# A fused SSM convolution and token-mixing MLP on one core: the hand-over from the last convolution chunk to the first four w1 blocks, rearranged

## The chip, the core and the metric

The kernel runs on one core of a Trainium2 chip. A core has a matrix engine (TensorE, "PE" in the profile, its weight loads "PEld"), VectorE ("DVE"), ScalarE ("ACT"), GpSimd ("POOL") and SyncE ("SP", here the queue that issues nearly all DMAs). Each engine works through its own queue in order. SBUF is the working memory of 128 partitions; PSUM receives the matmuls' results, here as four slots of two banks each (`pst0` to `pst3`). The metric is the time of one execution in microseconds (us), lower is better.

## The reference

One batch, S = 2048 tokens, D = 640 channels, F = 1728 hidden units, all float32:

```python
mod = (silu(c) @ w_mod)                       # six rows of 640: sa, ca, ga, sb, cb, gb
h = layernorm(x) * (1 + ca) + sa              # x = A_q, over the channels
kv = shift_conv(A_k, 4 taps) * A_v
y = causal_conv(kv, A_ssm_k) + kv * A_ssm_D   # length 2048, by FFT of length 4096, per channel
x = x + ga * (h * y)
h = layernorm(x) * (1 + cb) + sb
u = gelu(einsum("bsd,sf->bdf", h, w1) + b1)   # over the tokens
x = x + gb * (einsum("bdf,fs->bds", u, w2) + b2).transpose
```

## The kernel before

**First half.** The convolution works on five chunks of 128 channels (loop over `c`, L503). A chunk's transform has two stages in (`step1`, L208; `f2`, L222, eight groups g, multiplied with the kernel's transform by VectorE's `mul` and GpSimd's `add` into `Y`) and two stages out (`i2`, L253, two calls into `T2`, which lies in the tile `z`; `i1`, L268, two calls, one for each half of the 16 token rows j). A token row j is 128 tokens, one for each partition; `XH`/`XR(j)` (L83) hold x, rows 0 to 7 in tile `xa`, 8 to 15 in `xb`. `a1_ops` (L281) makes the first norm's rows in `A1` (ScalarE `ac`, then VectorE `po`), `gate` (L294) multiplies them with the result of `i1` in PSUM and adds to x, `spill` (L301) writes the chunk of x to DRAM (`xs`) for the end of the kernel. While `c` is worked on, `fill` holds loose VectorE work for the next chunks; in the last ones it is the statistics of finished chunks (`x1s`).

**Modulation.** `c @ w_mod` takes five pieces of 128 rows for three of the six rows at a time: `mod_load` (L339), `mod_part` (L343, six matmuls a piece, each two instructions, accumulated in `tap`, slot 3), `mod_sum` (L350) to SBUF, `mod_row` (L354), which spreads a row over the partitions and stores it (3: shift `SB`, 4: scale `CB`, 5: gate `GB`).

**Second half.** The first products contract over the tokens: `h` of the 16 rows j against w1 in 14 blocks of 128 hidden units. To reach float32 accuracy each operand is split in two parts of the type fp32r, `hi` (ScalarE copy) and `lo` (VectorE subtraction): `split_w` (L404) for weights, `H[j]` for h, and `mm` (L418) makes three products (hi hi, hi lo, lo hi), each in two halves of 320 columns, so six matmuls for a row and a block. Blocks 0 to 3 are accumulated together, row pair by row pair, since h comes into being only then; blocks 4 to 13 run afterwards on the finished `H`, one after the other (L796). Blocks then go through `u_evac` (L743), and the w2 products follow.

**Order around the change.** Everything is in the order written (`manual_schedule`, L53). In the last chunk (`c` = 4, `cn` None) after f2: the last two modulation pieces are loaded into `z`; block 0 (loaded in chunk 3 to `X`) is split, then `po`, three `mod_part`s, loads of blocks 1 to 3 (`aux`, `p`, `x`), `i2(0)`, splits of blocks 1 and 2, `i2(1)`, the last two `mod_part`s, split of block 3, load of block 4, `mod_sum`, `i1(0)`, `gate` of half 0, `i1(1)`, `mod_row(4)` and `(3)`. A w1 block is loaded by `load_w` (L390) for 128 columns of all 16 rows, 512 bytes at a time. Then (L698 on) the rows go through, a pair pr at a time: `x1_stats` (L659), a root by `rstd` (L308) or `rstd_pool` (L321: ScalarE's Sqrt, then a Newton step on GpSimd), `norm1` (ScalarE, into one of six pieces `tmp`), `mod_stats` (L668: times `CB`, plus `SB`, and the second norm's statistics, on VectorE), again `rstd_pool`, `norm2` (L678: the normed row and its `hi`), `rests` (its `lo`) and `products` (L691). The first norm's statistics are made for rows 0, 1, then 2 to 7, then 8 to 15 in one go each.

PSUM tiles come from `psum()` (L69), which goes round slots 0 to 2 in the first half and 0 to 3 from L655 on; a new tile on a slot, and a new tile on a memory tag (`mem`), waits until everything on the old one is done.

Of the kernel before, what the change touches and what calls it, by code (L numbers as in the profile page):

```python
# [49 lines left out]
def mixer_kernel(ctx: ExitStack, tc: tile.TileContext, q, k, v, shift_k, ssm_k, ssm_D, w1, b1, w2, b2, c,  # L50
# [16 lines left out]
    ring = [3]  # L67

    def psum():  # L69

        uid[0] += 1
        return psp.tile([128, 1024], F32, name=f"pst_{uid[0]}", tag=f"pst{uid[0] % ring[0]}", bufs=1)
# [9 lines left out]
    T_g, T_rows, T_t, sm = mem("g", 1280), mem("rows", 640), mem("t", 1280), mem("sm", 704)  # L82
# [24 lines left out]
    def small(n):  # L107
        so[0] += n
        assert so[0] <= 704
        return sm[:, so[0] - n:so[0]]  # L110
# [7 lines left out]
    msk = small(1)  # L118
    epsc = small(1)
# [133 lines left out]
    def i2(r):  # L253
# [9 lines left out]
        for qd in range(4):  # L263
            act.activation(T2[:, 8 * qd + 4 * r:8 * qd + 4 * r + 4].rearrange("p a m e -> p a e m"),
                           pp[qd // 2][:, 512 * (qd % 2):512 * (qd % 2) + 512].rearrange("p (a e m) -> p a e m",
                                                                                         a=4, e=2), AF.Copy)

    def i1(half):  # L268

        ps = psum()  # L270
# [10 lines left out]
    def a1_ops(c):  # L281
# [5 lines left out]
        if c == 0:  # L287
            def scaled(h):
                a, gh = A1[:, 8 * h:8 * h + 8], lambda G: G[:, None, 0:DC].to_broadcast([128, 8, DC])
# [4 lines left out]
    def gate(c, ps, half, eng=pool):  # L294
        a = A1[:, 8 * half:8 * half + 8]
        av = a.rearrange("p j (m e) -> p e j m", e=2)
        TT(dve, av, ps.rearrange("p (e j m) -> p e j m", e=2, j=8), av, ALU.mult)
        x = XH[half][:, :, DC * c:DC * c + DC]
        TT(eng, x, x, a, ALU.add)

    def spill(c):  # L301
        for half in range(2):
# [5 lines left out]
    def rstd(r, nm, j0, n):  # L308
# [3 lines left out]
        dve.tensor_scalar(v_, v_, EPS, None, op0=ALU.add)  # L312
        act.activation(t_, v_, AF.Sqrt)
        dve.reciprocal(r_, t_)
        TT(dve, t_, r_, r_, ALU.mult)
        TT(dve, t_, t_, v_, ALU.mult)
        dve.tensor_scalar(t_, t_, -0.5, 1.5, op0=ALU.mult, op1=ALU.add)
        TT(dve, r_, r_, t_, ALU.mult)
        dve.scalar_tensor_tensor(nm_, m_, -1.0, r_, op0=ALU.mult, op1=ALU.mult)

    def rstd_pool(r, nm, j0, n, between=None):  # L321

        m_, v_ = mv[:, j0:j0 + n, 0], mv[:, j0:j0 + n, 1]
        r_, nm_, t_ = r[:, j0:j0 + n], nm[:, j0:j0 + n], tm[:, j0:j0 + n]
        e_ = bst[:, j0:j0 + n, 4, 0]
        act.activation(t_, v_, AF.Sqrt, bias=epsc)
        pool.tensor_scalar(e_, v_, EPS, None, op0=ALU.add)
        pool.tensor_scalar(m_, m_, -1.0, None, op0=ALU.mult)
        if between:
            between()  # L330
        dve.reciprocal(r_, t_)
        TT(pool, t_, r_, r_, ALU.mult)
        TT(pool, t_, t_, e_, ALU.mult)
        pool.tensor_scalar(t_, t_, -0.5, 1.5, op0=ALU.mult, op1=ALU.add)
        TT(pool, r_, r_, t_, ALU.mult)
        TT(pool, nm_, m_, r_, ALU.mult)
# [17 lines left out]
    def mod_row(i, t):  # L354

        ps, j = psum().rearrange("p (h m) -> p h m", h=2), i % 3
# [4 lines left out]
        two = lambda t: t.rearrange("p (h m) -> p h m", h=2)  # L361
        if i == 0:
# [40 lines left out]

    def split_w(i, t2=None, eng=dve):  # L404
# [13 lines left out]
    def mm(ps, wh, wl, rh, rl, first, last):  # L418
# [581 lines left out]
```

## Time and profile before

| what | value |
|---|---|
| three runs | 741.24 us median, 734.45 to 748.20 |
| profiled execution | 737.33 us, span 735.5 us, mean granted TensorE clock 0.955 |
| PE busy | 653.1 us (89%) |
| PEld busy | 630.5 us (86%) |
| DVE busy | 499.4 us (68%) |
| ACT busy | 299.5 us (41%) |
| POOL busy | 176.2 us (24%) |
| last f2 ends, first four w1 blocks end | 288.1 us, 404.4 us |

How to read it. The page shows one execution; times are us from the span's start, durations in group rows mean ns of one instruction. A row of a group or of the timeline reads: line, engine, operation, tile written <- tiles read, shape, count, busy time; in brackets or behind the bar the idle time in front of it and who ended it. Most VectorE and GpSimd work goes through the helper on L59, so those rows are told apart by their tiles. The float32 matmuls of the first half count as two instructions each, fp32r ones (L424) as one. "PEclk" is the share of full clock that TensorE was granted.

### The profile page before, as it was taken

What the parts mean: (1) busy time and instruction counts of PE and PEld (TensorE: products, weight loads), DVE (VectorE), ACT (ScalarE), POOL (GpSimd) and SP (SyncE); (2) the same over time, 40 slices, a digit from 0 to 9 for tenths busy, and PEclk for the clock granted to TensorE, in tenths of its full rate; (3) what the DMA queues carried; (4) which work ended last, traced back from release to release, by engine and by line L of the source; (5) the groups of instructions that cost most, each with busy time, mean ns of one, the idle gap of its engine ahead of it and who ended that gap; (6) DMA issues with size and microseconds to landing.
All of it is one profiled execution on the core that took longest, in us unless ns stands there. A gap on an engine that the chain in (4) does not pass through costs nothing.

```text
span 735.5 us, 20693 instructions
## 1 busy us (share of the span) xinstructions
PE 653.1 (89%) x9107; PEld 630.5 (86%) x9107; DVE 499.4 (68%) x857; ACT 299.5 (41%) x441; POOL 176.2 (24%) x176
## 2 busy tenths in 40 slices
PE   0797969999999989655899999999999989999997
PEld 0787749989989978544899999999999989999997
DVE  7756659969877548488994321231298958888886
ACT  0432465645646535425665512321235322333222
POOL 5197048626329047022440000000000000000000
PEclk9999889999999999657899999999999999999999
DMA  9989988445420174950000535335163333555410
GB/s 180 241 235 255 265 228 167 97 80 132 89 61 4 29 198 151 187 116 2 0 1 21 95 77 96 58 59 110 55 186 101 92 117 110 153 164 172 145 55 36
DMA packets 171921, 84.90 MB, mean 115 GB/s; under 512 B 88852, under 2 KB 165431, under 8 KB 171831
## 3 DMA queue, kind: packets, MB, share of 16 engines
q1 hardware_dynamic: 167282, 82.26, 45.5%
q10 hardware_dynamic: 4548, 1.31, 1.1%
q8 instruction: 71, 1.16, 0.7%
q14 instruction: 20, 0.16, 0.1%
HBM read 73.07 MB, written 10.49 MB: 114 GB/s over the span
## 4 chain that ended last, share of the span: by engine, by line
PE 58%; DVE 22%; issue 6%; DMA 4%; POOL 4%; ACT 3%; SPq 2%; ACTq 0%; DVEq 0%; POOLq 0%
PE pst L424 26%; PE pst L216 9%; PE pst L941 7%; PE pst L232 6%; DVE m_w L59 4%; PE pst L261 4%; POOL y L59 3%; PE pst L277 3%; DVE m_x L59 3%; DVE tap L59 3%; DVE kt L59 2%; ACT m_w L854 2%; PE pst L866 2%; DVE m_x L875 1%; DVE m_v L59 1%
## 5 line engine op out<-in xcount | busy, mean ns | idle before, releaser
L232 PE MATMUL pst<-z,w 128*64 128x64 f32 x2560 | 96.8, 241 | 11.7 <-ACT z L218 6.1
L232 PEld LDWEIGHTS pst<-z,w 128*64 128x64 f32 x2560 | 95.3, 142 | 13.6 <-ACT z L218 7.3
L424 PE MATMUL pst<-r_z,wb 128*128 128x320 f32 x504 | 82.9, 321 | 16.4 <-ACT r_z L685 11.3
L59 POOL TENSOR_TENSOR y<-p 128x256 f32<-128x256 f32 x72 | 90.4, 1304 | 26.8 <-DVE p L59 26.6
L424 PEld LDWEIGHTS pst<-r_z,wb 128*128 128x128 f32 x504 | 79.1, 198 | 18.3 <-ACT r_z L685 12.5
L59 DVE TENSOR_TENSOR p<-pst,kt 128x512 f32<-128x512 f32 x80 | 52.7, 690 | 28.5 <-ACT kt L236 19.3
L216 PE MATMUL pst<-v,x 128*64 128x128 f32 x640 | 46.0, 303 | 23.6 <-DVE x L59 23.6
L218 ACT ACTIVATE z<-pst 128x1024 f32<-128x1024 f32 x40 | 45.8, 1146 | 48.6 <-PE pst L216 28.4
L216 PEld LDWEIGHTS pst<-v,x 128*64 128x64 f32 x640 | 44.0, 221 | 24.2 <-POOL t L449 23.6
L424 PE MATMUL pst<-h_x,wb 128*128 128x320 f32 x336 | 51.1, 309 | 0.0
L424 PEld LDWEIGHTS pst<-h_x,wb 128*128 128x128 f32 x336 | 49.7, 188 | 0.0
L236 ACT ACTIVATE kt<-pst 128x512 f32<-128x512 f32 x40 | 25.2, 630 | 59.4 <-PE pst L232 38.8
L261 PEld LDWEIGHTS pst<-v,y 32*128 32x128 f32 x1280 | 42.6, 204 | 6.8 <-issue 2.6
L261 PE MATMUL pst<-v,y 32*128 32x64 f32 x1280 | 44.7, 291 | 4.2 <-DVE y L59 1.4
L746 ACT ACTIVATE pst<-pst,sm 128x640 f32<-128x640 f32 x14 | 10.7, 767 | 86.1 <-PE pst L424 86.1
L59 DVE TENSOR_TENSOR wb<-x,wb 128x1024 fp32r<-128x1024 f32 (+1 forms) x32 | 36.8, 1188 | 12.0 <-ACT wb L413 11.9
L866 PE MATMUL pst<-r_z,m_w 128*128 128x320 f32 x222 | 42.8, 312 | 1.9 <-DVE m_w L59 1.4
L216 PE MATMUL pst<-v,p 128*64 128x128 f32 x640 | 37.8, 274 | 2.4 <-issue 2.4
L854 ACT ACTIVATE m_w<-m_v 128x896 fp32r<-128x896 f32 x24 | 22.2, 950 | 42.4 <-DVE m_v L59 29.5
L424 PE MATMUL pst<-h_a,wb 128*128 128x320 f32 x252 | 38.8, 309 | 0.0
L424 PE MATMUL pst<-r_v,wb 128*128 128x320 f32 x252 | 38.8, 309 | 0.0
L216 PEld LDWEIGHTS pst<-v,p 128*64 128x64 f32 x640 | 35.2, 137 | 3.6 <-issue 3.2
(213 smaller groups left out, 1272.2 us busy)
## 6 DMA issues: line engine op xcount, KB each, us to landing
x<-in_B_w_dram SPq DMA_DIRECT2D x24, 512.0 KB
m_v<-in_B_w_dram SPq DMA_DIRECT2D x15, 384.0 KB
x<-in_B_w_dram SPq DMA_DIRECT2D x14, 384.0 KB
aux<-in_A_ssm_k_dram SPq DMA_DIRECT2D x10, 512.0 KB
in<-in_A_k_dram SPq DMA_DIRECT2D x36, 128.0 KB
in<-in_A_v_dram SPq DMA_DIRECT2D x36, 128.0 KB
m_x<-xs SPq DMA_DIRECT2D x28, 160.0 KB
out_dram<-m_x SPq DMA_DIRECT2D x28, 160.0 KB
```

What stands on the lines that cost most here:

```text
L59: TT = lambda eng, o, a, b, op: eng.tensor_tensor(o, a, b, op=op)
L216: pe.matmul(ps[64 * ri:64 * ri + 64, o:o + 128], lhs, F1[:, 128 * ri:128 * ri + 128], start=True, stop=True)
L218: evac = lambda: act.activation(Z[:, side, t].rearrange("p a k e -> p e a k"), ps.rearrange("p (e a k) -> p e a k", a=8, e=2), AF.Copy)
L232: pe.matmul(ps[64 * h:64 * h + 64, o:o + 64], W2[k1 // 32][:, 2 * (k1 % 32) + ri], rhs, start=True, stop=True)
L236: act.activation(kt.rearrange("p (m i) -> p m i", i=32), pv[:, :, 1], AF.Copy)
L261: pe.matmul(pp[qd // 2][:, o:o + 64], Y[p, ri, i:i + 2].rearrange("p i k -> p (i k)"), V2[p, 64 * ri:64 * ri + 64], start=ri == 0, stop=ri ...
L277: pe.matmul(ps[64 * b:64 * b + 64, 512 * e + 64 * jj:512 * e + 64 * jj + 64], V1[p, ri, n2], T2[p, :, 32 * ri + n2], start=ri == 0, stop=r ...
L424: pe.matmul(ps[0:m, h, 0:320], w_.bitcast(F32R), r_[:, 320 * h:320 * h + 320].bitcast(F32R), start=first and i == 0, stop=last and i == 2)
L746: act.activation(p, p, AF.Gelu_apprx_tanh, bias=B1C[:, f:f + 1])
L854: act.activation(W[n][0].bitcast(F32R), a(w_), AF.Copy)
L866: pe.matmul(bank[n], w[:, i].bitcast(F32R), r.bitcast(F32R), start=i == 0 and k == 0, stop=i == 6 and k == 2)
L941: pe.matmul(acc[s][:, h, 0:320], w[:, f_].bitcast(F32R), u[r + h].bitcast(F32R), start=f_ == 0 and k == 0, stop=f_ == NF - 1 and k == 2)
```

## The change

It rearranges the last chunk and the four blocks; the computation and the number of w1 matmuls stay the same.

1. **Weights by rows.** `load_rows(r)` loads four token rows j = 4r to 4r+3 of blocks 0 to 3 at once, 2048 bytes at a time; `split_rows` splits them for chosen blocks. Rows 0 to 7 are loaded in chunk 3, rows 8 to 15 after the first half's gate, split in the pair loop. Blocks 0 and 1 take tiles `w0`, `w1`, block 3 `in`, block 2 `y`.
2. **Modulation.** Two pieces are loaded in chunk 3 instead of three; the third and fourth go to `z`, the fifth to `p`, all issued after f2. The third `mod_part` still stands ahead of `i2(0)`, the fourth stands between the two `i2`, the fifth after `i1(0)`. `CB` is stored by VectorE; `SB`'s ScalarE copy also sums it (`msb`).
3. **Last chunk's order.** The po of the last chunk is by halves, two of its four passes inside f2's groups 5 and 6. Two of the four copies of `i2(1)` go to VectorE. `i1(0)` is followed by the gate of rows 0 and 1 alone, their statistics, then the gate of rows 2 to 7; `i1(1)` comes after `mod_row(4)` and `(3)`, its gate after the second pair's products have begun.
4. **Second norms by sums.** Instead of bn_stats: a fused multiply by `CB` with a running sum gives the mean (`second`), a fused add subtracts it and adds `SB`, a ScalarE Square with a running sum gives the variance. The Square's result goes to the place of the row's `lo` and is overwritten. The normed row isn't stored any more: `hi` and `lo` are made from the centred row with the root as scale.
5. **Roots in one pass.** The roots of the second norm of a pair and of the first norm of a later pair are taken together (`root_in`: GpSimd and ScalarE; `root`: VectorE, Newton step in four instructions, `newton`).
6. **Products.** For pairs 0 to 6 the products with `hi` of both rows for all blocks come first, then those with `lo`; pair 0 leaves block 3 for later. Rows from 4 on are normed in place in x instead of `tmp`; statistics of later rows are made two or four at a time.

```diff
     def i2(r, eng=None):
...
+            if eng is not None and qd > 1:
+                eng.tensor_scalar(o, i, 1.0, None, op0=ALU.mult)
+            else:
+                act.activation(o, i, AF.Copy)
...
+    def newton(r, t, v, n=None):
+        dve.reciprocal(r, t)
+        dve.scalar_tensor_tensor(t, r, -0.5, r, op0=ALU.mult, op1=ALU.mult)
+        TT(dve, t, t, v, ALU.mult)
+        dve.scalar_tensor_tensor(r, t, 1.5, r, op0=ALU.add, op1=ALU.mult)
...
+    def load_rows(r, t):
+        for i in range(4):
+            sync.dma_start(t[:, 512 * i:512 * i + 512], dram(w1, (4 * r + i) * F, [[16 * F, 2], [32 * F, 64], [1, 512]]))
+
+    def split_rows(r, t, blocks, hi=True, lo=True):
+        j, t = slice(4 * r, 4 * r + 4), t.rearrange("p (j m) -> p j m", j=4)
+        for f in blocks if hi else ():
+            act.activation(blk[f][0][:, j].bitcast(F32R), t[:, :, 128 * f:128 * f + 128], AF.Copy)
+        for f in blocks if lo else ():
+            TT(dve, blk[f][1][:, j].bitcast(F32R), t[:, :, 128 * f:128 * f + 128], blk[f][0][:, j], ALU.subtract)
...
+            if cn is None and g in (5, 6):
+                run(po[:1])
+                po = po[1:]
...
         else:
-            for kk in range(3, 5):
-                mod_load(3, kk, pl[kk])
-            split_w(0)
-            run(po)
+            mod_load(3, 2, pl[2])
+            mod_load(3, 3, pl[3])
+            mod_load(3, 4, pl[4])
             for kk in range(3):
                 mod_part(tap, kk, three(pl[kk]))
-            load_w(1, T_aux[:, 0:2048])
-            load_w(2, P)
-            load_w(3, X)
+            split_rows(0, X, (0, 1, 3))
+            split_rows(1, T_aux[:, 0:2048], (0, 1, 3))
+            run(po)
...
             i2(0)
             if cn is None:
-                split_w(1)
-                split_w(2, mem("in", 4288, "wb2"))
+                mod_part(tap, 3, three(pl[3]))
+                i2(1, dve)
+                split_rows(0, X, (2,))
+                split_rows(1, T_aux[:, 0:2048], (2,))
+                break
...
+            pl = [T_in[:, 0:1920], T_in[:, 1920:3840], T_z[:, 0:1920], T_z[:, 1920:3840], P[:, 0:1920]]
+            for kk in range(2):
+                mod_load(3, kk, pl[kk])
+            load_rows(0, X)
+            load_rows(1, T_aux[:, 0:2048])
...
+    roots = (((), (0, 1)), ((0, 1), (2, 3)), ((2, 3), (4, 5)), ((4, 5), (6, 7, 8, 9)), ((6, 7), (10, 11)),
+             ((8, 9), (12, 13)), ((10, 11), (14, 15)), ((12, 13), ()), ((14, 15), ()))
...
+    def root_in(n):
+        second_, first_ = roots[n]
+        o = start[n]
+        if second_:
+            pool.tensor_scalar(V_[:, o:o + 2], V_[:, o:o + 2], 1 / D, EPS, op0=ALU.mult, op1=ALU.add)
+            o += 2
+        if first_:
+            pool.tensor_scalar(V_[:, o:start[n + 1]], mv[:, first_[0]:first_[-1] + 1, 1], EPS, None, op0=ALU.add)
+        act.activation(T_[:, start[n]:start[n + 1]], V_[:, start[n]:start[n + 1]], AF.Sqrt)
...
+    def second(pr):
+        for j in (2 * pr, 2 * pr + 1):
+            t = row(j)
+            dve.scalar_tensor_tensor(t, t, 1.0, CB, op0=ALU.mult, op1=ALU.mult, accum_out=su[:, j:j + 1])
+        n = su[:, 2 * pr:2 * pr + 2]
+        dve.tensor_scalar(n, n, msb, -1 / D, op0=ALU.add, op1=ALU.mult)
+        for j in (2 * pr, 2 * pr + 1):
+            t = row(j)
+            dve.scalar_tensor_tensor(t, t, su[:, j:j + 1], SB, op0=ALU.add, op1=ALU.add)
+        for j in (2 * pr, 2 * pr + 1):
...
+            act.activation(H[j][1].bitcast(F32R), row(j), AF.Square, accum_out=at(V_, 2, j))
+
+    def halves(pr):
+        for j in (2 * pr, 2 * pr + 1):
+            act.activation(H[j][0].bitcast(F32R), row(j), AF.Identity, scale=at(R_, 2, j))
+
+    def rests(pr):
+        for j in (2 * pr, 2 * pr + 1):
+            dve.scalar_tensor_tensor(H[j][1].bitcast(F32R), row(j), at(R_, 2, j), H[j][0], op0=ALU.mult, op1=ALU.subtract)
...
+    ps0 = i1(0)
+    mod_part(tap, 4, three(pl[4]))
+    gate(NC - 1, ps0, 0, dve, 0, 2)
+    x1_stats(range(2))
+    mod_sum(tap, T_t[:, 0:640])
+    root_in(0)
+    gate(NC - 1, ps0, 0, dve, 2, 8, (lambda: root(0),))
+    spill(NC - 1, (0,))
+    mod_row(4, T_t[:, 0:640], s2)
+    norm1(0)
+    mod_row(3, T_t[:, 0:640], 3)
+    ps = i1(1, s1)
+    gb = mod_row(5, T_t[:, 0:640], s2, True)
...
+    for r, t in ((2, X), (3, P)):
+        load_rows(r, t)
+    second(0)
+    x1_stats(range(2, 4))
+    root_in(1)
+    gb()
+    root(1)
+    halves(0)
+    norm1(1)
+    rests(0)
+    products(0, range(3))
+    x1_stats(range(4, 6))
+    second(1)
+    gate(NC - 1, ps, 1, dve, then=(lambda: root_in(2), lambda: root(2), lambda: halves(1), lambda: norm1(2)))
+    spill(NC - 1, (1,))
+    products(0, [3])
+    rests(1)
+    products(1)
+    second(2)
+    x1_stats(range(6, 10))
+    root_in(3)
+    root(3)
+    halves(2)
+    norm1(3)
+    rests(2)
+    norm1(4)
+    products(2)
+    split_rows(2, X, range(4))
+    for pr in range(3, 8):
+        second(pr)
+        if pr > 3:
+            rests(pr - 1)
+            products(pr - 1)
+        if pr == 5:
+            split_rows(3, P, range(4))
+        if pr < 6:
+            x1_stats(range(2 * pr + 4, 2 * pr + 6))
+        root_in(pr + 1)
+        root(pr + 1)
+        halves(pr)
+        if pr < 6:
+            norm1(pr + 2)
+        if pr == 3:
+            load_w(4)
+    rests(7)
     products(7)
```

More of the change, by code (lines that the diff above doesn't have):

```diff
@@ L361, in mod_row @@
         two = lambda t: t.rearrange("p (h m) -> p h m", h=2)
+        if later:
+            return lambda: act.activation(two(GB), ps, AF.Copy)
         if i == 0:
@@ L618, in mixer_kernel @@
             ps = i1(half)
[L619 to L621 removed]
+            if c and half:
                 dv(3)
```

243 lines of the change are left out of this document (98 added, 145 removed).

## The prediction

> **What bounds the kernel now.** I read the page's slices first, then the chain that ended last, then the timeline of each engine and the busy time by stretches, for 286 to 405 us. The slices show where TensorE is neither busy nor at full clock: slices 16 to 19 of 18.4 us, some 294 to 368 us.
>
> ```profile
> PE   0797969999999989655899999999999989999997
> PEclk9999889999999999657899999999999999999999
> ```
>
> The chain, in order of time (start, length, what), names what ends each wait there.
>
> ```profile
> 293.01 3.39 SPq L396
> 296.44 8.34 DMA p<-in_B_w_dram
> 304.79 3.01 issue
> 307.88 2.00 ACT wb L413 x2
> ...
> 311.96 6.55 PE pst L277 x255
> ...
> 321.30 0.18 DVE sm L314
> ...
> 352.49 87.58 PE pst L424 x576
> ```
>
> So the second `i2` is computed by 304.2, but its copies out of PSUM stand on ScalarE behind the splits of w1 blocks 1 and 2, which wait for loads issued only at 291 to 299; `i1` starts at 311.96. Then VectorE's rows carry the chain, and from 352.49 TensorE is the bound: what starts its products earlier is worth something, what VectorE does beside them is not, while it keeps up. TensorE's own rows:
>
> ```profile
> 288.06 2.35 PE L347 MATMUL tap<-in,sm 128*32 128x320 f32 x24
> 291.42 4.09 PE L261 MATMUL pst<-v,y 32*128 32x64 f32 x132
> 304.11 4.00 PE L347 MATMUL tap<-z,sm 128*32 128x320 f32 x24
> 338.40 8.46 PE L424 MATMUL pst<-r_z,wb 128*128 128x320 f32 x46 [0.96 <-DVE r_z L59]
> 352.49 6.23 PE L424 MATMUL pst<-r_z,wb 128*128 128x320 f32 x22 [4.23 <-DVE r_z L59]
> 379.76 10.74 PE L424 MATMUL pst<-r_z,wb 128*128 128x320 f32 x72
> 404.42 2.80 PE L424 MATMUL pst<-r_z,wb 128*128 128x320 f32 x18
> ```
>
> The four blocks are 384 matmuls: 50 before 352.49, the rest until block 4 starts at 404.42. At full clock one takes 10.74/72 = 0.149 us, so a pair of rows (48) 7.16 us; at 352.49 it takes 0.283. Busy time in windows of 3.41 us shows why (second column PE busy, then weight load, DVE, ACT, POOL; then the granted clock):
>
> ```profile
> 293.83:297.24 3.41, 2.40 (x85) 2.27 (x80) 3.38 (x3) 1.92 (x4) 0.00 (x0) 1.00 1.14 272
> 297.24:300.65 3.41, 3.18 (x60) 2.99 (x57) 1.13 (x1) 0.26 (x1) 0.00 (x0) 0.50 1.21 204
> 304.07:307.48 3.41, 3.41 (x24) 1.32 (x24) 2.16 (x2) 0.72 (x1) 0.00 (x0) 0.50 1.21 205
> 307.48:310.89 3.41, 0.63 (x9) 0.02 (x3) 1.93 (x2) 3.01 (x5) 0.00 (x0) 1.00 0.93 162
> ```
>
> The clock is 1.00 or 0.50 through a whole window, set by the window before: 2.40 us busy lost it, 3.18 (of `i2`) didn't bring it back, 3.41 did.
>
> **The change, part 1: up to `i1(0)` in PSUM.** Before, VectorE gets it at 315.71; call that t0.
>
> ```profile
> 315.71 1.23 DVE L59 TENSOR_TENSOR aux<-pst,aux 128x1024 f32<-128x1024 f32 x1 [0.28 <-PE pst L277]
> 253.73 2.10 PE L277 MATMUL pst<-z,v 64*64 64x64 f32 x128
> 310.29 1.62 ACT z L264 x3
> ```
>
> Removed: the ScalarE queue's wait for w1. The rows of w1 for j 0 to 7 (2.1 MB) are issued behind the third spill, with two modulation loads instead of three and instead of block 0: 4.1 MB instead of 4.0, from about 268 on, needed from 289.5. SP is idle after them until 288.18, so they cost nothing there. Added: the third modulation piece now goes to `z`, which f2 reads until 288.06, and TensorE must have it before `i2(0)`; before, it lay in `aux` long since. Everything behind it on TensorE waits.
>
> ```profile
> 288.18 0.90 SPq L340 DMA_DIRECT2D z<-in_w_mod_dram  x2
> 289.00:292.46 3.46, 3.46 (x65) 1.92 (x60) 3.46 (x5) 2.49 (x4) 1.54 (x2) 1.00 0.90 285
> 294.90:300.10 5.20, 4.20 (x96) 4.06 (x92) 3.44 (x2) 2.17 (x4) 0.00 (x0) 0.73 1.20 208
> 302.78 2.00 ACT L413 ACTIVATE wb<-aux 128x1024 fp32r<-128x1024 f32 x2 [5.28 <-DMA aux<-in_B_w_dram]
> ```
>
> The first 0.98 MB of such a load have moved by 292.46 (last column: 285 GB/s). How long after its last byte a load can be used: w1's block 1 (1.05 MB at 208 GB/s behind the two z loads) has moved by 300.1 and is used at 302.78, 2.7 us. The ends are 1 and 2.7; I take 2.7, the only row: 295.2. TensorE idles from 290.4 (its two ready pieces done) to 295.2 and loses its clock at 293.83. Then twelve matmuls of the piece, 2.0 us (24 in 4.00), to 297.2; `i2(0)`, 128 matmuls at 4.09/132 = 0.031 us, twice that at half clock. The window from 297.24 is wholly busy, so I let the clock return at 300.65, as it did at 307.48: 57 matmuls cold, 71 warm, done at 302.9. The fourth piece, 1.2, goes beside ScalarE's copies (0.54 each); `i2(1)` 4.1, to 308.1; its four copies, now two on ScalarE and two on VectorE, 1.35 instead of 2.1; `i1(0)`, 128 matmuls, 2.1. So t0 = 311.6, or 4.1 earlier. Ends: cold throughout, 295.2 + 24.1 (2.0 + 7.6 + 2.0 + 7.6 + 1.4 + 3.5) = 319.3; never cold and the piece usable at 293.5, 293.5 + 13.9 = 307.4. [...]
>
> Hidden here: the splits of blocks 0, 1, 3 (six of 512 elements on each engine, done by 296), the two VectorE passes of po put into f2's last turns (they delay f2's last sums by some 0.4) and the other two (by 298.5): cover is the wait until 295.2. If that went, 0.5 us. The load into `p` waits on SP for those sums; nothing is queued behind it until the spill.
>
> **Part 2: from t0 to the first product.** Before, 22.7 us (338.40 - 315.71). Prices of one instruction:
>
> ```profile
> L59 DVE TENSOR_TENSOR t_g<-t_g,kt 128x640 f32<-128x640 f32 x12 | 9.8, 813 | 0.2
> L875 DVE SCALAR_TENSOR_TENSOR m_x<-m_x,sm 128x320 f32<-128x320 f32 x6 | 3.3, 545 | 0.0
> L59 DVE TENSOR_TENSOR m_x<-m_x 128x320 f32<-128x320 f32 x35 | 17.2, 492 | 1.2
> L59 DVE TENSOR_TENSOR wb<-x,wb 128x1024 fp32r<-128x1024 f32 x24 | 28.4, 1222 | 11.0 <-ACT wb L413 10.9
> L59 DVE TENSOR_TENSOR p<-pst,kt 128x512 f32<-128x512 f32 x80 | 52.7, 690 | 28.5 <-ACT kt L236 19.3 <-POOL y L59 8.8 <-POOL aux L59 0.3
> L662 DVE BATCH_NORM_AGGREGATE sm<-sm 128x2 f32<-128x30 f32 x16 | 4.7, 292 | 0.6
> L502 DVE BATCH_NORM_STATS2 sm<-xb 128x6 f32<-128x128 f32 x40 | 8.8, 271 | 0.0
> L666 ACT ACTIVATE t_g<-xa,sm 128x640 f32<-128x640 f32 x2 | 1.7, 912 | 4.9 <-POOL sm L59 4.9
> L685 ACT ACTIVATE r_v<-t_p 128x640 fp32r<-128x640 f32 x2 | 1.5, 743 | 0.1
> L327 POOL TENSOR_SCALAR sm<-sm 128x2 f32<-128x2 f32 x6 | 4.1, 683 | 24.9 <-DVE sm L676 24.9
> ```
>
> A fused pass of 640 elements: 0.81 plus 0.05 (545 - 492), 0.86; where it also sums, the trace has no row: as without (0.74, back to back) to 1.5 if it went at half rate; I take 0.86, next to the fused row. A small one 0.2, a root on VectorE (four steps and the mean) 1.0, statistics of a row 0.48 (0.27 + 0.29, overlapping), a Square between L685 and L666, 0.80. `second` of a pair is then 4 x 0.86 + 0.2 = 3.6, `rests` 1.6.
>
> In us after t0: gate of two rows 0.9, statistics 1.85, ScalarE's sum of the pieces and root 2.85, VectorE's root (after the gate's product for the other six) 3.9, norm of pair 0 until 5.7; row 4 (the scale), evacuated on VectorE, 5.65; `second(0)` to 9.25; Squares to 10.1 (`z` is free only when `i1(1)` has read it, about 8.5); GpSimd's sum and ScalarE's root 10.95; VectorE's root 12.0; first half 12.7. The first product is at 12.7 instead of 22.7, since the big gate(1), six rows' statistics and GpSimd's chain of five no longer stand in front of it.
>
> **Part 3: the pace behind it.** Before, VectorE has a pair done every 6.96 us, under TensorE's 7.16:
>
> ```profile
> 353.15 1.68 DVE L59 TENSOR_TENSOR t_p<-t_p,kt 128x640 f32<-128x640 f32 x2
> 360.11 1.68 DVE L59 TENSOR_TENSOR t_g<-t_g,kt 128x640 f32<-128x640 f32 x2
> ```
>
> After, a pair costs VectorE 3.6 + 1.6 + 0.95 (statistics of two later rows, before the stream before) + 1.0 = 7.15, and eight splits of 512 elements, 0.65 each, go in between: the lead gets eaten. Followed on: pair 1's half at 22.65, products of pairs 0 and 1 (96) from 12.7 to 30.0, cold at first; pair 2 from 32.6, after statistics of four rows, to 39.8. Now row split 2: its ScalarE halves stand behind the norms of pairs 3 and 4 (until 36.75), VectorE idles from 34.2 to 37.35 for them, splits to 39.95, does `second(3)` to 43.55 and gets a root at 46.65: half of pair 3 at 47.3. TensorE idles 7.5 us and starts cold again, 2.4 more. Pair 3 ends at 56.8, pair 4 at 64.0; pair 5 from 65.55 to 72.7, pair 6 to 79.9, pair 7 to 87. Before it was 88.7 (404.42 - 315.71). The spill of half 1 (23.2) lands before norm(4) overwrites those rows at 35; row loads 2 and 3 (eight DMAs between the spills) land long before 36.75.
>
> **The sum.** 311.6 + 87 = 398.6 against 404.4, 5.8 us less. Behind it nothing changes: TensorE bounds, block 4's load is issued in time. The profiled execution took 737.33 (span 735.5), 3.9 under the median 741.24 of the three runs, which spread over 2%: about what this kernel's measurement can tell from no change. Forecast 731.5.
>
> **Rivals.** (a) Slower: the fused form with two SBUF operands runs at half rate. By the slope of the rows above (1222 - 690 over 512, 1.04 ns) each costs 0.67 more, six a pair 4.0: VectorE, already level with TensorE, becomes the bound from the third pair, 8 x 4.0 = 32, to 763.5. It decides from 0.5 us an instruction on (0.5 x 48 = 24). The 545 row, with two SBUF operands and no doubling, is against it; if only the summing ones (16) are slow, 10.7 more, 742. [...] (b) Slower: Square and Sqrt don't share a table, two loads a pair:
>
> ```profile
> L313 ACT ACT_TABLE_LOAD x1 | 1.3, 1283 | 0.0
> ```
>
> nine roots, 2.6 each, 23: 754.5; half of it if one is hidden. Sqrt, Copy and Identity alternate now with one load in all, which says nothing of Square. (c) The wait isn't cured but moved: the piece's load at 295.2 and half clock through both `i2`, t0 319.3: 739.2. For it, the 3.18 window. (d) Faster: the piece usable at 293.5, no cold window (t0 307.4), and the chain at its short ends, summing at no price (-1.9), GpSimd at 0.25 a step while VectorE is between passes (-3), ScalarE's passes at 0.7 (-2): 80; 387.4, 17 less, 720.3.
>
> **How the numbers follow.** Forecast 0.40, (d) 0.24, (c) 0.19, (a) 0.06 and its half 0.05, (b) 0.06. Faster than 2% is (d) and 0.06 of the forecast's own tail (722 to 740): 0.30. Slower is (a), two thirds of (b) and 0.03 of tails: 0.13. Within 2%: 0.57. The range runs from below (d), 717, to above (c) and the half of (a), 748.
>
> **What would show it.** TensorE waiting from 290.4 for a DMA into `z` until about 295, with a window at 0.50 behind it; `i1` no longer behind splits; the first L424-like product some 13 us after `i1(0)`; TensorE idle for 2 to 8 us between pairs 2 and 3; VectorE 90% busy between. Wrong if fused passes take over 1.2 us, if table loads stand between Squares and roots, or if TensorE has no gap after the first product.

## The result, and the profile after

The change makes the kernel slower: 780.95 us median (778.10 to 783.53, four runs) against 741.01 (734.45 to 748.20, four runs), a ratio of 1.0569, 95% interval 1.0484 to 1.0654. Forecast were 731.5 us, with a range to 748. The profiled execution took 782.42 us, with a span of 780.4, 44.9 more than before's 735.5; by the start of w1 block 4 (404.42 before) it is 44.7 late, so the whole loss lies in the stretch that was changed.

First the page's slices of the changed kernel, of 19.5 us each (span / 40).

```profile
PE   0897679989999990387508999999999998999997
PEclk9999979999998995578959999999999999999999
DMA  9989996172410331501130054425235253554320
```

There are two holes in TensorE's row: slices 15 and 16 (293 to 332 us; slice 15 is empty) and slice 20 (390 to 410 us). The DMA row says why: at slice 15, while TensorE does nothing, the 16 DMA engines are one tenth busy. So it isn't bandwidth that is short (from 316 to 321 us they move 291 GB/s). The stretch 306 to 310 us by itself (columns: TensorE, weight loads, VectorE, ScalarE, GpSimd busy, the clock, the DMA share and GB/s):

```profile
306.00:310.00 4.00, 0.00 (x0) 0.00 (x0) 0.00 (x0) 0.00 (x0) 0.00 (x0) 0.50 0.13 51
```

No engine works, and DMA runs at a share of 0.13 and 51 GB/s. A share of 0.13 is about 2/16, as if two DMA engines were at it and fourteen idle (the experiments test this). What they carry stands in SP's timeline (start, length, what):

```profile
271.65 13.38 SPq L402 DMA_DIRECT2D x<-in_B_w_dram  x4
285.13 20.57 SPq L402 DMA_DIRECT2D aux<-in_B_w_dram  x4
305.80 6.76 SPq L335 DMA_DIRECT2D z<-in_w_mod_dram  x2
...
361.58 20.57 SPq L402 DMA_DIRECT2D p<-in_B_w_dram  x4
382.26 7.55 SPq L311 DMA_DIRECT2D xs<-xb  x2
```

These are the new `load_rows` (L402). Each of its DMAs moves 256 KB, which at 51 GB/s is 5.1 us, and 20.57/4 is 5.1: SP stands on each further issue for as long as one load takes, and what comes behind them on SP stands too: `z`'s modulation piece, issued at 305.80 instead of 288.18, and the spill of x's last half, at 382.26. Nor is `z` quick once issued: its load takes 18.21 us (in e1, below, it is used 4.95 us after its issue), and at 306 to 310 us the share is still 0.13, as if the row loads ahead of it drain first. The chain of waits of the changed kernel runs through exactly these two places.

```profile
300.71 4.99 SPq L402
305.80 18.21 DMA z<-in_w_mod_dram
...
382.26 4.97 SPq L311
387.28 9.95 DMA xs<-xb
```

On the engines it shows as follows (TensorE, then ScalarE; in brackets the idle time before and what ended it):

```profile
324.06 2.35 PE L342 MATMUL tap<-z,sm 128*32 128x320 f32 x12 [32.24 <-DMA z<-in_w_mod_dram]
326.34 7.10 PE L263 MATMUL pst<-v,y 32*128 32x64 f32 x128
409.02 11.11 PE L431 MATMUL pst<-h_a,wb 128*128 128x320 f32 x64 [25.92 <-ACT h_a L719]
449.11 2.90 PE L431 MATMUL pst<-r_z,wb0b 128*128 128x320 f32 x18 [0.89 <-DVE u_x L59]
```

```profile
321.83 1.67 ACT L407 ACTIVATE wb<-aux 128x512 fp32r<-128x512 f32 x3 [21.48 <-DMA aux<-in_B_w_dram]
397.31 1.73 ACT L699 ACTIVATE xb<-xb,sm,kt 128x640 f32<-128x640 f32 x2 [19.25 <-DMA xs<-xb]
```

The wait of 25.92 says "ACT h_a", but ScalarE is itself waiting: its norm of row 8 overwrites x in place and may not until the spill has read it. The balance (t0 is VectorE's first piece of the gate, as in the prediction):

| us | predicted | after | with the loads on all engines (e1, below) |
|---|---|---|---|
| t0 | 311.6 | 343.8 | 311.9 |
| t0 to the first product | 12.7 | 12.6 | 12.6 |
| TensorE's gap after pair 2 | 7.5 | 25.9 | 5.0 |
| t0 to block 4 | 87 | 105.3 | 86.0 |

So 32.2 us are lost ahead of t0 and 18.3 behind it, and these two are the miss.

### The profile page after: what moved, and what is told of

It is laid out like the page before. It is cut to its first block, busy times and chain, and to the rows that moved or that the text cites. A ratio compares the mean times of both kernels' runs of the same rounds, so it can differ in the third digit from the quotient of the medians.

```text
span 780.4 us, 20703 instructions
## 1 busy us (share of the span) xinstructions
PE 651.4 (83%) x9107; PEld 629.0 (81%) x9107; DVE 493.1 (63%) x861; ACT 297.4 (38%) x461; POOL 155.5 (20%) x135
## 3 DMA queue, kind: packets, MB, share of 16 engines
q8 instruction: 71, 1.16, 0.7%
## 4 chain that ended last, share of the span: by engine, by line
PE 49%; DVE 21%; SPq 9%; DMA 8%; issue 5%; POOL 4%; ACT 4%; ACTq 0%; DVEq 0%; POOLq 0%
PE pst L431 20%; PE pst L218 7%; PE pst L1015 6%; SPq L402 6%; PE pst L234 5%; PE pst L263 5%; DVE m_w L59 4%; POOL y L59 4%; DVE m_x L59 3%; DMA z<-in_w_mod_dram 2%; PE pst L282 2%; DVE tap L59 2%; ACT m_w L928 2%; DVE kt L59 2%; PE pst L940 2%
## 5 line engine op out<-in xcount | busy, mean ns | idle before, releaser
L59 POOL TENSOR_TENSOR y<-p 128x256 f32<-128x256 f32 x72 | 92.4, 1328 | 27.0 <-DVE p L59 26.6
L218 PEld LDWEIGHTS pst<-v,x 128*64 128x64 f32 x640 | 44.7, 221 | 24.4 <-POOL t L456 23.4
L263 PE MATMUL pst<-v,y 32*128 32x64 f32 x1280 | 44.9, 296 | 2.1 <-DVE y L59 1.5
L940 PEld LDWEIGHTS pst<-r_z,m_w 128*128 128x128 f32 x222 | 34.8, 188 | 5.0 <-DVE m_w L59 4.0
L59 DVE TENSOR_TENSOR tap<-tap,kt 128x512 f32<-128x512 f32 x51 | 35.6, 697 | 1.3
L59 DVE TENSOR_TENSOR kt<-in,tap 128x512 f32<-128x512 f32 x51 | 35.0, 687 | 1.4
L282 PE MATMUL pst<-z,v 64*64 64x64 f32 x1280 | 26.3, 244 | 10.5 <-DMA v<-in_const_v_dram 6.8
L282 PEld LDWEIGHTS pst<-z,v 64*64 64x64 f32 x1280 | 24.5, 158 | 13.0 <-issue 10.8
L431 PE MATMUL pst<-h_a,wb 128*128 128x320 f32 x72 | 12.5, 337 | 25.9 <-ACT h_a L719 25.9
L431 PEld LDWEIGHTS pst<-h_a,wb 128*128 128x128 f32 x72 | 12.1, 212 | 26.2 <-ACT h_a L719 26.2
```

What stands on the lines that cost most here:

```text
L59: TT = lambda eng, o, a, b, op: eng.tensor_tensor(o, a, b, op=op)
L218: pe.matmul(ps[64 * ri:64 * ri + 64, o:o + 128], lhs, F1[:, 128 * ri:128 * ri + 128], start=True, stop=True)
L263: pe.matmul(pp[qd // 2][:, o:o + 64], Y[p, ri, i:i + 2].rearrange("p i k -> p (i k)"), V2[p, 64 * ri:64 * ri + 64], start=ri == 0, stop=ri ...
L282: pe.matmul(ps[64 * b:64 * b + 64, 512 * e + 64 * jj:512 * e + 64 * jj + 64], V1[p, ri, n2], T2[p, :, 32 * ri + n2], start=ri == 0, stop=r ...
L431: pe.matmul(ps[0:m, h, 0:320], w_.bitcast(F32R), r_[:, 320 * h:320 * h + 320].bitcast(F32R), start=first and i == 0, stop=last and i == 2)
L940: pe.matmul(bank[n], w[:, i].bitcast(F32R), r.bitcast(F32R), start=i == 0 and k == 0, stop=i == 6 and k == 2)
```

## The experiments

**Is it the number of DMA engines?** In `load_rows` the source's outermost dimension counts the two blocks of 64 partitions: `[16F,2],[32F,64],[1,512]`. That 2 and the trace's share of 0.13, about 2 of 16 engines, agree; that the one brings the other was the author's estimate. e1 moves the same bytes with 64 partitions outermost:

```diff
-for i in range(4):
-    sync.dma_start(t[:, 512*i:512*i+512],
-                   dram(w1, (4*r+i)*F, [[16*F,2],[32*F,64],[1,512]]))
+for b in range(2):
+    sync.dma_start(t[64*b:64*b+64].rearrange("p (i m) -> p i m", i=4),
+                   dram(w1, (16*b+4*r)*F, [[32*F,64],[F,4],[1,512]]))
```

> Edit: each of the four row loads is issued as two DMAs of 64 partitions and four rows (512 KB, 2 KB runs), partitions outermost, instead of four DMAs of 128 partitions whose source begins with a dimension of 2. Theory E (a row load runs on only 2 of the 16 DMA engines: share 0.13 = 2/16, 51 GB/s, 5 us a DMA, and SP's queue stands behind them): SP issues a DMA in about 0.65 us, the rates rise above 200 GB/s, z lands at about 295 instead of 324, i1(0) reaches VectorE at about 315 (295.2 and the 19.75 us that the changed kernel takes from there), the four blocks end 87 us later, at 402; time 735, the same as the kernel before within 1%. Rival P (rows 221 KB apart are slow to read whatever the number of engines): the rates stay near 50 GB/s and the time above 770. Rival S (the stall is not in the loads but in the new order of the stage): loads fast, time still above 755.

Measured: 735.97 us (731.02 to 742.33, ten runs), ratio to before 0.9955 (0.9916 to 0.9994). The 45 us are gone by this alone. Its rows on SP, TensorE and VectorE:

```profile
268.50 1.34 SPq L402 DMA_DIRECT2D x<-in_B_w_dram  x2
269.96 1.27 SPq L402 DMA_DIRECT2D aux<-in_B_w_dram  x2
293.22 0.98 SPq L335 DMA_DIRECT2D z<-in_w_mod_dram  x2
```

```profile
287.05 6.14 PE L234 MATMUL pst<-z,w 128*64 128x64 f32 x134 [3.65 <-issue]
293.12 2.35 PE L342 MATMUL tap<-in,sm 128*32 128x320 f32 x24
298.17 1.28 PE L342 MATMUL tap<-z,sm 128*32 128x320 f32 x12 [2.70 <-DMA z<-in_w_mod_dram]
299.38 3.80 PE L263 MATMUL pst<-v,y 32*128 32x64 f32 x128
357.71 11.69 PE L432 MATMUL pst<-h_a,wb 128*128 128x320 f32 x64 [5.03 <-ACT h_a L720]
397.82 2.92 PE L432 MATMUL pst<-r_z,wb0b 128*128 128x320 f32 x18 [0.90 <-DVE u_x L59]
```

```profile
311.86 0.42 DVE L59 TENSOR_TENSOR aux<-pst,aux 128x256 f32<-128x256 f32 x1 [0.75 <-PE pst L282]
```

SP is through with rows 0 to 7 in 2.7 us instead of 34, the DMA share is 0.97 to 1.08 from 268 to 284 us, and t0 is 311.86 where 311.6 was predicted (how much of that is luck, see below).

**Which half costs what.** e2 has the form of e1 for rows 0 to 7 alone, e3 (with `r > 1`) for rows 8 to 15 alone; against the change:

```diff
 def load_rows(r, t):
+    if r < 2:
+        for b in range(2):
+            sync.dma_start(t[64*b:64*b+64].rearrange("p (i m) -> p i m", i=4),
+                           dram(w1, (16*b+4*r)*F, [[32*F,64],[F,4],[1,512]]))
+        return
     for i in range(4):
```

> Edit: only the loads of rows 0 to 7 (chunk 3) are changed as in the run before. Theory E: i1(0) at about 315 instead of 343.8; behind it the loads of rows 8 to 15 still hold the second spill on SP, so the norm of rows 8 and 9 still starts some 53 us after i1(0) and TensorE still idles some 26 us there; the blocks end 105 us after i1(0), at 420; time 752 to 755. Rivals P and S: above 770.

> Edit: only the loads of rows 8 to 15 (after the first half's gate) are changed. Theory E: z still lands at 324 and i1(0) reaches VectorE at 344; then the spill of half 1 goes out at once, TensorE's gap after pair 2 shrinks from 26 us to about 7.5, the blocks end 87 us after i1(0), at 431; time 762 to 765. With the run before it adds up to the first one's gain. Rivals: no change, 780.

Measured: e2 756.61 us, ratio 1.0222 (1.0158 to 1.0286); e3 760.95, ratio 1.0281 (1.0218 to 1.0343). Against 780.95, medians of different batches, that is 24.3 and 20.0 less, together 44.3 of the 45.0 that e1 wins: the two losses are separate and add. e2 keeps the gap after pair 2, e3 the wait for z (first line e2, second e3):

```profile
382.19 12.24 PE L436 MATMUL pst<-h_a,wb 128*128 128x320 f32 x64 [24.48 <-ACT h_a L724]
```

```profile
321.55 2.35 PE L342 MATMUL tap<-z,sm 128*32 128x320 f32 x12 [32.52 <-DMA z<-in_w_mod_dram]
```

**Is it only that the outer dimension is small?** e4 cuts e1's DMA of 64 partitions into 62 and 2. If a large outer dimension is enough, the 62 move about as fast as e1's 64.

```diff
 for b in range(2):
-    sync.dma_start(t[64*b:64*b+64].rearrange("p (i m) -> p i m", i=4),
-                   dram(w1, (16*b+4*r)*F, [[32*F,64],[F,4],[1,512]]))
+    for p, n in ((0, 62), (62, 2)):
+        sync.dma_start(t[64*b+p:64*b+p+n].rearrange("p (i m) -> p i m", i=4),
+                       dram(w1, (16*b+4*r+32*p)*F, [[32*F,n],[F,4],[1,512]]))
```

> Edit: as in the first run, but each DMA of 64 partitions is cut into one of 62 and one of 2; pattern, run length, row distance and bytes are those of the first run. [...] Rival A (it was the two-level source of the 128-partition DMA that was slow, or the number of bytes in a DMA): as fast as the first run, 735.

Measured: 791.34 us, one run. SP stands for 21.10 us on the loads of rows 4 to 7, and DMA runs at the same 0.13 and 51 GB/s:

```profile
294.15 21.10 SPq L403 DMA_DIRECT2D aux<-in_B_w_dram  x4
```

```profile
296.00:310.00 14.00, 0.00 (x0) 0.00 (x0) 1.90 (x3) 1.67 (x3) 0.00 (x0) 0.50 0.13 51
```

With 62 partitions outermost the share is 0.13, as with 2, where 64 have 0.97 to 1.08: a large outer dimension isn't enough. What sets the share for other counts these runs don't show.

**The rows' own lateness, or the queue behind them?** e9 and e10 leave the loads on two engines and move what stands behind them on SP to another queue: e9 the z loads to ScalarE's (first lines), e10 the last spill to GpSimd's (last two).

```diff
-mod_load(3, 2, pl[2])
-mod_load(3, 3, pl[3])
+mod_load(3, 2, pl[2], act)
+mod_load(3, 3, pl[3], act)
...
-spill(NC - 1, (1,))
+spill(NC - 1, (1,), pool)
```

> The changed kernel with its row loads on two engines left as they are (781 us), but the two modulation loads into z are issued on ScalarE's queue, where no row load stands ahead. It parts what the early 32 us of delay (t0 at 343.8 instead of 311.6) are made of: z standing in SP's queue, or rows 4 to 7 themselves coming late. Theory queue alone: z is usable by 296 and t0 comes back to about 312; the time is 749. Theory data as well: the rows 4 to 7 still land at about 321 (the last of them is issued at 305.8 in the changed kernel and used at 321.83), ScalarE's splits of them end at 323.5, the copies of the first i2 out of PSUM stand behind those on ScalarE, and t0 is 333.6, ten earlier only; the time is 771. I expect the second.

> The changed kernel with its row loads left on two engines, but the spill of the last half of x is issued on GpSimd's queue instead of SP's, where it stands behind 31 us of row loads. It parts the late delay (TensorE's gap after pair 2: 25.9 us where 5.0 are left with the loads on all engines) in the same way. Theory queue alone: the spill lands some 5 us after VectorE's sum, the norm of row 8 waits for nothing, rows 8 to 11 land by about 375 (issued from 350.7 on, some 5 us each and one outstanding), 5 us ahead of their splits; the gap is 5 to 8 us and the time 762. Theory data: the rows themselves, or the spill's share of the two busy engines, come 10 us and more too late; the gap stays above 15 us and the time at 772 to 781. I expect the first.

Measured: e9 777.25 us, ratio 1.0493 (1.0333 to 1.0654); e10 765.75, ratio 1.0338 (1.0184 to 1.0491). First e9's TensorE and ScalarE, then e10's GpSimd and TensorE:

```profile
298.56 2.35 PE L342 MATMUL tap<-z,sm 128*32 128x320 f32 x12 [7.81 <-DMA z<-in_w_mod_dram]
327.41 7.09 PE L263 MATMUL pst<-v,y 32*128 32x64 f32 x124 [16.55 <-ACT z L271]
```

```profile
324.66 1.67 ACT L407 ACTIVATE wb<-aux 128x512 fp32r<-128x512 f32 x3 [19.57 <-DMA aux<-in_B_w_dram]
```

```profile
368.46 1.60 POOL L311 DMA_DIRECT2D xs<-xb  x2 [2.75 <-DVE xb L59]
```

```profile
391.43 12.08 PE L431 MATMUL pst<-h_a,wb 128*128 128x320 f32 x64 [6.56 <-ACT h_a L719]
```

Ahead of t0 the queue is the smaller part: in e9 z is there at 298.56, yet rows 4 to 7 still come at 324.66, and the copies of the first i2 stand behind their splits on ScalarE; t0 is 339.7, only 4.1 earlier (I had said 10; both i2 then ran at half clock, 7.11 us for the first and 7.09 for 124 matmuls of the second). Behind t0 it is all: with the spill out of SP's queue the gap falls from 25.92 to 6.56 (6.57 in e3, whose rows 8 to 15 are on all engines), t0 to block 4 takes 85.9 us, as in e1 (86.0), and rows 8 to 15 themselves come in time.

**What is left on e1's path.** The prediction had the third modulation piece (z) ahead of the first i2 and row split 2 behind two norms. e5 puts the piece between the two i2 and the fourth behind them, e6 puts split 2's ScalarE halves ahead of pair 1's second norm, e7 does both (e5's lines first).

```diff
-for kk in range(3):
+for kk in range(2):
     mod_part(tap, kk, three(pl[kk]))
...
 i2(0)
-mod_part(tap, 3, three(pl[3]))
+mod_part(tap, 2, three(pl[2]))
 i2(1, dve)
+mod_part(tap, 3, three(pl[3]))
...
 norm1(1)
+split_rows(2, X, range(4), lo=False)
...
-split_rows(2, X, range(4))
+split_rows(2, X, range(4), hi=False)
```

> Base: the kernel with both loads of rows on all engines (735.97 us). The third modulation piece, whose load into z can only start when f2 has read z, goes from ahead of the first i2 to between the two, and the fourth piece behind the second i2. Theory: in the base the first i2 stands behind that piece (TensorE waits 2.70 us for z, then 1.28 of matmuls) though its own input (VectorE's last sum into y) is there some 3.2 us sooner; t0 comes 3.0 us earlier (308.9 on the base's clock) and the time is 733, ratio to before 0.991. Rival: TensorE's wait for z is not on the path, since VectorE's sums and copies set it: t0 moves under 1 us and the time stays at 736. Second rival: TensorE idles long enough ahead of i2 to lose its clock for both i2 (7.1 instead of 3.9 us each): t0 5 us later, 741.

> Base as in e5. ScalarE's four halves of the third row split (2.17 us) are emitted ahead of the second norm of pair 1, where ScalarE idles 3.0 us, instead of behind the norms of pairs 3 and 4. Theory, the prediction's step of part 3: VectorE's wait of 2.81 us for those halves goes, TensorE's gap after pair 2 falls from 5.03 to 2.2 us, and the time by 2.7, to 733.3. Rival: the rows are not in SBUF yet at that place, ScalarE waits for them, pair 1 comes later by what it waits (1 to 3 us), and the time stays at 736 or rises to 738.

> Both edits of e5 and e6 on the same base. If each moves its own part of the path they add: 730.3, ratio to before 0.986. If VectorE is the bound behind them, as its 90% busy share in that stretch allows, the gain of the second is eaten by later gaps between pairs and the time is 733.

Measured, each against the kernel before: e5 735.62 us, 0.9915 (0.9878 to 0.9951); e6 737.77, 0.9908 (0.9872 to 0.9945); e7 726.53, 0.9806 (0.9768 to 0.9843). (The kernel before, run alongside, had a median of 741.34 here and 739.9 beside e1, so the ratios are what compares.) e5 and e6 can't be told from e1 by these intervals; e7 can. For e5 a t0 of 308.9 was expected; its own trace has 316.3, for there both i2 run slow (5.13 and 7.11 us), as its second rival has it. In e7's trace the gap after pair 2 is 2.20 us where e1 has 5.03 and e5, without the edit, 5.08, which was the expected size; e6's is 3.67:

```profile
353.98 7.33 PE L432 MATMUL pst<-h_a,wb 128*128 128x320 f32 x48 [2.20 <-ACT h_a L721]
```

The gap alone also depends on how fast pair 2 itself ran (7.33 us in e6, 8.80 in e7). From pair 2's first product to pair 3's it is 13.9 us in e1 and e5 and 11.0 in e6 and e7, so the place of split 2 is worth 2.9 us in these traces. What of the rest of e7's gain is the order of the pieces and what the clock (next) isn't settled: in e5's own profiled execution the second i2 took 7.11 us, in e7's 4.8.

**What brings the clock back.** The prediction let a window wholly full of i2 restore the clock. In the changed kernel, where TensorE starts cold at 324.06, two such windows did not (behind the five busy times of a row stands the granted clock):

```profile
326.80:330.20 3.40, 3.40 (x72) 3.40 (x72) 0.00 (x0) 0.00 (x0) 0.00 (x0) 0.50 0.08 27
330.20:333.60 3.40, 3.40 (x67) 3.25 (x66) 0.00 (x0) 0.12 (x1) 0.00 (x0) 0.50 0.00 0
333.62:337.04 3.42, 3.42 (x40) 1.76 (x34) 0.00 (x0) 2.01 (x4) 0.00 (x0) 0.50 0.00 0
337.04:340.45 3.41, 3.08 (x108) 2.94 (x104) 0.23 (x1) 0.29 (x1) 0.00 (x0) 0.99 0.02 5
```

It came back behind the window with a modulation piece (twelve matmuls of 128 rows, 2.35 us) in it. e8 is the changed kernel with the fourth piece put ahead of the first i2, so 24 such matmuls come first.

```diff
-for kk in range(3):
+for kk in range(4):
     mod_part(tap, kk, three(pl[kk]))
...
 i2(0)
-mod_part(tap, 3, three(pl[3]))
```

> The changed kernel as it is (row loads on two engines, 781 us) with the fourth modulation piece moved ahead of the first i2, so that behind the long wait TensorE starts with 24 matmuls of 128 rows instead of 12. Two accounts of the clock. One: what brings it back is a window in which matmuls that fill the array run, and i2's, which use 32 rows, count too little; then the clock is back after the window that these 24 fill, some 3 to 7 us after the start, and most of i2 runs at 1.00 (the first in under 6 us instead of 7.10, the second in 3.9 instead of 4.5). Other: the clock needs three windows of any busy work; then the first i2 takes 7.1 us again and the clock is back some 13 us after the start, as in the changed kernel. The time is 778 to 781 either way.

Measured: 782.94 us, one run, and the first account:

```profile
324.66:328.07 3.41, 3.37 (x21) 0.58 (x12) 1.44 (x2) 0.00 (x0) 0.00 (x0) 0.50 0.11 44
328.07:331.48 3.41, 3.41 (x119) 3.41 (x116) 0.00 (x0) 0.00 (x0) 0.00 (x0) 0.93 0.02 5
331.48:334.90 3.42, 2.42 (x85) 2.29 (x83) 0.00 (x0) 2.14 (x4) 0.00 (x0) 1.00 0.00 0
```

```profile
328.07 4.22 PE L263 MATMUL pst<-v,y 32*128 32x64 f32 x132
```

The clock is back at about 328.5, 5 us after the start instead of 13, and the 132 matmuls from 328.07 on, the whole first i2 among them, take 4.22 us where the changed kernel's first i2 took 7.10. The second i2, expected at 3.9, took 5.24: TensorE was busy for only 2.42 us of the window from 331.48, and the clock was lost again (0.57 in the window from 334.90). The busy time alone doesn't settle that: in the kernel before, windows with 1.91 and 2.18 us busy (from 259.69 and 266.52) were each followed by one at 1.00. Here a window with 3.37 us of matmuls of 128 rows brought the clock back, and two with 3.40 us of i2's 32 rows at half clock didn't. The two kinds differ in columns too (64 and 320). The matmuls of i1 (64 rows, and 64 columns like i2's) help to part that. In e6's trace both i2 had run slow and TensorE had idled for 1.53 us; then i1 ran alone, and behind it twelve matmuls of a piece took 1.28 us, the time at full clock, where they take 2.35 at half:

```profile
320.53 3.48 PE L282 MATMUL pst<-z,v 64*64 64x64 f32 x128 [1.53 <-DVE z L269]
323.94 1.28 PE L342 MATMUL tap<-p,sm 128*32 128x320 f32 x12
```

So it isn't the number of columns that i2 lacks; that rows count is the likeliest reading, but the shapes of the weights differ as well, and no run varies rows alone. A piece by itself isn't enough either: in e11 (below) twelve matmuls of 128 rows stand at 300.79 between the two i2, and the second i2 still takes 7.11 us; how much of a window they must fill wasn't measured. At full clock a window of i2 held it (331.48 is at 1.00).

**A stand that came with the faster loads.** e1's row at 287.05 has TensorE standing 3.65 us in f2 on "issue", that is on nothing that the profile shows; with another of 1.35 at 278.50 it is 5.0, where the kernel before has 0.2 and the changed one none. It is there (4.0 to 5.0) in e1, e2, e5, e6 and e7, whose row loads fill the DMA engines just before, and not (0.3 at most) in e3, e4, e8, e9 and e10. In e1 the longer part runs from 283.4 to 287.05, mostly behind the loads: the share is 1.02 from 280 to 284 and 0.07 from 284 to 288. In all five it falls on the same matmul of f2, the 379th of 512. A window of e1, and below it the same one of the changed kernel:

```profile
280.00:284.00 4.00, 3.40 (x92) 3.25 (x89) 4.00 (x11) 1.78 (x4) 3.55 (x3) 1.00 1.02 214
```

```profile
280.00:284.00 4.00, 4.00 (x115) 4.00 (x112) 4.00 (x16) 2.83 (x6) 4.00 (x4) 1.00 0.15 55
```

e11 is e7 with rows 4 to 7 loaded behind z instead of ahead of f2; e12 is e11 with VectorE's two passes over `aux` (`po`), which the change had put into f2's last turns, back behind f2 (last three lines).

```diff
 load_rows(0, X)
-load_rows(1, T_aux[:, 0:2048])
...
 mod_load(3, 3, pl[3])
+load_rows(1, T_aux[:, 0:2048])
...
-split_rows(1, T_aux[:, 0:2048], (0, 1, 3))
 run(po)
...
 i2(0)
+split_rows(1, T_aux[:, 0:2048], (0, 1, 3))
...
-if cn is None and g in (5, 6):
-    run(po[:1])
-    po = po[1:]
```

> Base: the kernel with both edits, pieces and halves (726.53 us). The load of rows 4 to 7 is issued behind the two loads into z instead of ahead of f2, and its splits for blocks 0, 1 and 3 stand behind the first i2's copies on ScalarE. In every kernel with the early row loads on all engines TensorE stands for 4 to 5 us in f2 on nothing but its own instructions, while the 16 DMA engines are busy without a gap from 272 to 284; in the kernels whose DMAs leave room then it stands for 0.3 us at most. Theory: the filled DMA engines hold up what the engines' instructions come by; with only 2 MB ahead of f2 the stand goes, f2 ends 4 to 5 us sooner (its pieces begin at 288 to 289 instead of 293.25), the rows land by about 299, ahead of their splits, and the time is 722, ratio to before 0.974. Rival: the stand has to do with the order of instructions and stays at 4 us, the time stays at 726 to 727. Second rival: the stand goes, but the rows, now behind z, land after 303 and hold the copies of the second i2; the time stays at 726 or more.

> Base: the kernel with the later rows 4 to 7 (731.24 us), where f2 ends 5 us sooner and the first i2 still starts at 293.91, for VectorE's sum into y is late: the two passes over aux that the change put into f2's last turns (1.22 and 3.96 us) stand ahead of it, TensorE idles 3.24 us, and both i2 run at half clock (6.95 and 7.11 us). This kernel undoes that one part: the two passes go back behind y, where VectorE has room until the second i2. Theory: y is there by 291.5, TensorE idles under 1.5 us, the clock stays, the two i2 take some 4 us each, t0 comes from 315.8 to about 306, and the time is 722 (ratio to before 0.974). Rival: the clock is lost all the same, at the pause of 1 to 1.5 us or in the wait for z, and both i2 take 7 us; t0 is then 313 and the time 729 to 731.

Measured: e11 731.24 us, 0.9874 (0.9842 to 0.9907); e12 724.96, 0.9796 (0.9757 to 0.9836). e11, then e12:

```profile
283.38 5.00 PE L234 MATMUL pst<-z,w 128*64 128x64 f32 x134 [0.36 <-issue]
293.91 6.95 PE L263 MATMUL pst<-v,y 32*128 32x64 f32 x128 [3.24 <-DVE y L59]
```

```profile
286.58 3.96 DVE L59 TENSOR_TENSOR aux<-aux,g 128x1024 f32<-128x1024 f32 x1
```

```profile
287.59 3.19 PE L263 MATMUL pst<-v,y 32*128 32x64 f32 x93 [0.52 <-DVE y L59]
294.11 2.40 PE L263 MATMUL pst<-v,y 32*128 32x64 f32 x35 [3.32 <-issue]
```

```profile
292.00:296.00 4.00, 1.89 (x34) 1.89 (x34) 2.53 (x3) 0.00 (x0) 0.00 (x0) 0.52 1.05 223
```

In e11 the stand went as expected and f2's ready pieces began at 288.3 instead of e7's 293.25, but the time rose: VectorE's pass over `aux` took 3.96 us where the same pass took 1.85 in e7 (why, no row shows), y came late, TensorE idled 3.24 us, lost its clock and ran both i2 at half. In e12 y comes at once, and the stand is back, 3.32 us, now in i2, where the moved loads fill the engines (share 1.05), and the second i2 runs at half clock (7.11 us); that takes back what was won: t0 is 310.7, as in e7 (311.0), instead of the expected 306. So the stand moves with the row loads from f2 to i2. Filled engines alone don't make it: in the kernel before the shares of 1.14 to 1.21 from 293.8 to 307.5 us go with a stand of 0.92 us (at 301.34), and in e11, with 1.05 to 1.07 from 292 to 300, none shows, though TensorE was waiting for y until 293.91. The page counts instruction packets among the DMA's (q8: 71, 1.16 MB in e1); that instructions come late for it is a guess that no row shows, and the cause stays open. e12 and e7 can't be told apart, and both are the fastest kernels here, some 2% under before.

## Why the prediction was wrong

- **The failed step** is in part 1, of rows 0 to 7: "SP is idle after them until 288.18, so they cost nothing there." It counted bytes (4.1 MB instead of 4.0) and not engines; SP wasn't idle but stood on them until 305.80, and t0 came 32.2 us late. The same error stands in part 3: the spill of half 1 "lands before norm(4) overwrites those rows at 35; row loads 2 and 3 [...] land long before 36.75". The spill was issued at t0+38.5 only, and the gap was 25.9 instead of 7.5. What the runs show in its place: the loads move at 51 GB/s with a DMA share of 0.13 (about two engines of 16), SP stands about 5.1 us on each, and z and the spill wait behind them. e1 shows the one cause of both, and no rival named it: all rivals took the loads as hidden.
- **t0 with the loads cured**: 311.6 predicted, 311.9 in e1, but by errors that cancel, which is luck. The two ready pieces ended at 295.5 instead of 290.4 (the stand), z was usable 4.95 us after its issue instead of 7.0, and i2(0) ran at full clock, where 57 cold matmuls were expected. That half clock comes in other executions: e2, with the same wait for z (2.76), ran its first i2 in 7.11 us, and e6, which is e1 up to t0, both (an execution of 741.93 us). Rival (c), half clock in i2, is thus probably part of e1's spread (granted clock 0.966 in its run of 731.0 us, 0.954 in the one of 741.8), and letting a window of i2 end it was wrong (two of 3.40 us in the changed kernel didn't).
- **From t0 to the first product**: right, 12.7 against 12.6 in both kernels, and step by step: in e1 `second(0)` is done 9.1 us after t0 (9.25 predicted), VectorE's root 11.7 (12.0).
- **The pace behind it**: right in kind. VectorE waits for split 2's halves (2.81 us at 348.29 in e1), TensorE's gap is 5.0, block 4 starts at t0+86.0 where its products were to end at t0+87, and e6 and e7 show that order as the cause of 2.9 us.
- **The two passes in f2's last turns**, costed at 0.4 us: true where f2 is late anyway. In e11, where it isn't, taking them out gives 6.3 us (e12), by way of y and the clock of the first i2.
- **Rival (a)**, the fused form at half rate, is refuted. The summing pass takes 0.82 us, the other 0.88, the plain one had 0.81 (groups of the changed kernel by line: busy us, mean ns):

```profile
L705 DVE SCALAR_TENSOR_TENSOR xb<-xb,kt 128x640 f32<-128x640 f32 x8 | 6.3, 821 | 0.0
L710 DVE SCALAR_TENSOR_TENSOR xb<-xb,sm,kt 128x640 f32<-128x640 f32 x8 | 6.7, 882 | 0.1
```

```profile
445.00 1.28 ACT L819 ACT_TABLE_LOAD   x1
```

- **Rival (b)**, table loads between Square and Sqrt, is refuted: between the Squares and the roots there is none; the next is the Gelu's, the last line above.
- **The sum**: 731.5 forecast for a change whose loads cost nothing; e1, which is that change, has 735.97, and 0.9955 (0.9916 to 0.9994) of before. The 5.8 us were taken from one execution of 737.33; taken from the median of 741.24 they give 735.4. By block 4 e1's profiled execution is 6.6 us ahead of before's (397.82 against 404.42).

## What to carry to other kernels

Of a moved or reshaped load look not only at the bytes but at the outermost dimension: with 2 or 62 there the DMA share was 0.13 here (2/16, 51 GB/s), with 64 it was 0.97 to 1.08, and whatever stood behind the load on the issuing queue waited as well. In these profiles a share that stays at 0.13 while everything idles was the sign of it. And with TensorE near full, what an edit frees can be lost again to the clock: a pause of 3.24 us ahead of the two i2 cost some 6 us more in e11 (14.1 us for both, 7.7 in e1).

## What the runs showed of the hardware that was not expected

- At a DMA share of 0.13 (about two engines of 16) the loads moved 51 GB/s, and with loads in flight the issue of a further one on the same queue took as long as one of them (5.1 us for 256 KB, changed kernel).
- The read of the accumulator behind a summing pass has a row of its own (0.08 us on VectorE, 0.19 on ScalarE), but the next pass didn't wait for it: two Squares in e1 start 0.74 us apart (320.31 and 321.05), and one takes 0.74.
- Where the row loads filled the DMA engines (share 1.02 in e1, 1.05 in e12) or had just done so, TensorE stood without a named wait, 3.65 us in f2 of e1 and 3.32 in i2 of e12; the cause is open.
- A window filled with matmuls of 32 rows at half clock didn't bring the clock back (two of 3.40 us in the changed kernel); matmuls of 128 rows did (3.37 us of a window of e8, then 0.93), and so did matmuls of 64 rows and 64 columns (3.48 us in e6, then a piece in 1.28).
